# Attention slices spread over a block of feed-forward, engine latency in the planner, and a new order for the last output unit

## The chip, the cores and the metric

The kernel runs on one core of a Trainium2 chip. The metric is the device time of one execution in microseconds (us), as the median of a few runs. The engines are named as in the profile: PE is the tensor engine's matmul, PEld its weight loads, DVE the vector engine, ACT the scalar engine, POOL GpSimd, and SP the engine whose queue issues most stores.

## The reference

Linear attention of 8 batches, 8 heads, 576 tokens and 64 columns per head, normed, and then a bilinear feed-forward layer over all 4608 tokens:

```python
kv  = np.einsum('bhsd,bhse->bhde', k, v)
out = np.einsum('bhsd,bhde->bhse', q, kv)
rms = np.sqrt(np.mean(out * out, axis=-1, keepdims=True) + 1e-06)
x   = (out / rms * g_norm)            # (8, 8, 576, 64), then as (4608, 512)
a, b = x @ w_a, x @ w_b               # 512 x 1536 each
result = (a * b) @ w_out              # 1536 x 512
```

## The kernel before, in words

The feed-forward layer runs over nine blocks of 512 tokens. Block 0 is computed plainly (`std_block`, and `o_std` for its output in four products of 128 tokens, L815). Blocks 1 to 8 use Winograd's form of a 2x2 matrix product: seven products instead of eight, at the price of sums. In `wino_block` a block has six units `j`, each with the products p1 to p7 (four matmuls of 256 columns each, two for w_a and two for w_b, L718), evictions by ACT (`ev`, L411, to `u` or `c`), sums by DVE (`comb`, L737, to `c`), and a product a*b by DVE (`mul`, L771, to `abt`). Ahead of a block, DVE computes four differences of the normed tokens, m3, m1, m2 and m4 (`t_op`, L687, to `T` and `xp`), each of which reads the one before. The output of a block, `o_unit`, is the same form again: four sums of `abt` in two chunks (L866, to `as` and `abt`, a chain of four per chunk), seven products (L881, twelve matmuls each, in two pieces of six, in the last unit in six of two), evictions (L915) and sums (L921) to `o_sb`, and stores by SP (L788). It is worked off within the next block.

Attention of batch b makes the tokens that the blocks read. `load_node` brings q, k and v by GpSimd's DMAs, one batch behind the other (a copy to `gate_t`, L551, waits for the batch before), and a transposing DMA on SP makes `qT` (L570). `late_batch` copies the keys to another order (`kr_t` from `k_t`, L512, on DVE), multiplies keys and values (L521), and then works off eight slices, one for each pair of heads and half of the tokens: a matmul (L340), a square on ACT (L350), a matmul with ones (L354), a reciprocal root on ACT (L358), and a multiplication on DVE that writes the tokens to `xp` (L363).

All this is put in order by a planner when the program is built. Each piece of work is a `Node` with an engine, a duration, a priority, dependencies, and the buffers that it takes and frees; `Plan.order` then takes, again and again, the node that could start first by its own reckoning, and within 0.06 us the one with the smaller priority. The program's instructions stand on each engine in that order, and the engines run them in it. A dependency across engines counts with a latency from the table `LAT`; one on the same engine counts with none. The priority of a batch's work comes from its window, `at_win[b]`, two times between which its slices are spread evenly; `st` are the reckoned starts of the blocks. PSUM's banks go round in rings: 0 to 3 for the products (`RX`, `RY`), 4 for the output (`RO`), 5 to 7 for attention (`RQ`, `RS`).

Of the kernel before, what the change touches and what calls it, by code (L numbers as in the profile page):

```python
# [69 lines left out]

class Plan:
    LAT = {"PE": 0.27, "SP": 2.2, "ACT": 0.2, "DVE": 0.18}

    def __init__(self, t0):
        self.t0, self.nodes = t0, []
# [15 lines left out]
    def ready(self, n):  # L91
        t = 0.0
        for d, lat in n.deps:
            if d.end is None:
                return INF
            t = max(t, self.after(d, 0.0 if lat is None and d.eng == n.eng else lat))
        for b in n.takes:
            t = max(t, b.ring.when(), b.ring.pool.pick()[0])
        return t
# [35 lines left out]
def kernel(  # L135
# [11 lines left out]
    nc = tc.nc  # L147
# [10 lines left out]
    NCH = S // 128  # L158
# [275 lines left out]

    blocks_of = [(0, N0)] + [(t, t + 2 * n) for t, n in BLOCKS]
    readers = {}
    o_reads = []

    def slices(at, win, extra):
        w0, w1 = win  # L440
# [57 lines left out]
    def late_batch(b, load, win):  # L498
        at = Attn(b)
        w0, w1 = win  # L500
        kb, vb, qb = load["k"], load["v"], load["q"]
        kr, kd = Buf(RKR), Buf(RKD)
        at.qt = [qb, kd]

        def view(t):
            return t[:, 0 : H * (NCH + 1) * D].rearrange("p (h c d) -> p h c d", h=H, d=D)

        s = Buf(RS)

        r = plan.add(  # L510
            "DVE", 0.75, w0,
            lambda: nc.vector.tensor_copy(kr.tile[:], view(kb.tile).rearrange("p h c d -> p c h d")),  # L512
            [(load["n"], load["k_us"])], [kr], [kb],
        )

        def kv_mm():
            kv_ps = s.tile[:].rearrange("p (a e) -> p a e", a=NP)
            for c in range(NCH + 1):
                for p in range(NP):
                    hs = slice(2 * p, 2 * p + 2)  # L520
                    nc.tensor.matmul(  # L521
                        kv_ps[:, p, :],
                        lhsT=kr.tile[:, c, hs, :],
                        rhs=view(vb.tile)[:, hs, c, :],
                        start=(c == 0 and p == 0),
                        stop=(c == NCH and p == NP - 1),
                    )

        n = plan.add(
            "PE", 1.15, w0, kv_mm, [r, (load["n"], load["kv_us"]), plan.at(w0 - 3)], [s, kd], [kr, vb]  # L530
        )

        def kv_out():
            kv_ps = s.tile[:].rearrange("p (a e) -> p a e", a=NP)
            at.kvd = kd.tile
            nc.scalar.copy(at.kvd[0:D, :, 0:D], kv_ps[0:D, :, 0:D])
            nc.scalar.copy(at.kvd[D:, :, D:], kv_ps[D:, :, D:])
            for p in range(NP):
                at.q[p] = qb.tile[:, p, :]

        m = plan.add("ACT", 0.75, w0, kv_out, [n], (), [s])
        slices(at, (w0 + 0.12 * (w1 - w0), w1), lambda p: [m, (load["qn"], 5.5)])
# [127 lines left out]
    def wino_block(bi, win, wsum):  # L670
# [26 lines left out]
        for j in range(NJ):  # L697
# [16 lines left out]
            def pe(off, ps, lhs, rhs, start, deps, takes=(), frees=()):  # L714
                def prod():
                    for i, (w, sm) in enumerate(wts):
                        for kc in range(2):
                            nc.tensor.matmul(  # L718
                                ps.tile[:, i * n : (i + 1) * n],
                                lhsT=lhs(w, sm)[:, kc, :],  # L720
                                rhs=rhs()[:, kc, :],
                                start=start and i == 0 and kc == 0,
                                stop=kc == 1,
                                skip_group_check=True,
                            )

                return plan.add("PE", mm_us(4, n), pr + off, prod, deps, takes, frees)
# [13 lines left out]
            def w_at(kc, fs):  # L741
                return lambda w, sm: w[:, kc : kc + 2, fs]
# [4 lines left out]
            s1, s2, s3, s4 = ([wsum[w, j][i] for w in "ab"] for i in range(4))  # L747
            p1 = pe(0.0, X, w_at(0, fs), lambda: b11, True, xdeps(lo, t0, t0 + n), [X])
            e1 = ev(0.0, u1, X, p1)
            p2 = pe(0.1, Y, w_at(2, fs), lambda: b21, True, xdeps(hi, t0, t0 + n), [Y])  # L750
            c11 = comb(0.1, 0, 0, Y, u1, [p2, e1], [Y, u1])
            p6 = pe(0.2, X, s_at(0), lambda: tt(t2), False, [e1, m2] + s2, (), [t2])
            e2 = ev(0.2, u2, X, p6)
            p5 = pe(0.3, Z, w_at(0, f2), lambda: b12, True, [m1] + s1, [Z])
            p7 = pe(0.4, X, s_at(1), lambda: tt(t3), False, [e2, m3] + s3, (), [t3])
            e3 = ev(0.4, u3, X, p7)
            c22 = comb(0.4, 1, 1, Z, u3, [p5, e3], [u3])
# [16 lines left out]
            muls[j] = muls[j + NJ] = m  # L774
        return ab, muls

    def store(g0, o_sb):
        i = 0
        while i < 128:
            b, j = divmod(g0 + i, S)  # L780
            if b < NE:
                c, sp = divmod(j, EP)
                n = min(128 - i, EP - sp)
                r0, st = b * S + EC * sp + c, EC
            else:
                n = min(128 - i, S - j)
                r0, st = b * S + j, 1
            nc.sync.dma_start(out=out[r0 : r0 + st * (n - 1) + 1 : st, :], in_=o_sb[i : i + n, :])  # L788
            i += n

    def o_block(bi, ab, muls, osum, win, chunks, rings, pieces):
# [48 lines left out]
    def o_unit(r0, ab, muls, osum, pr, du, chunks, pieces, m, w, first, second, X, Y, Z, ob, s2, s3, s4, W):  # L840
# [83 lines left out]
                "DVE", dve_us((subs.stop - subs.start) * EH), pr + off * du, add, deps, (), frees  # L924
            )

        def put(fi, subs, deps, us=0.45):
            def go():
                for i in range(subs.start, subs.stop):
                    store(r0 + (fi * m + i) * 128, ob.tile[:, fi * m + i])  # L930

            plan.add("SP", us * (subs.stop - subs.start), pr + 7 * du, go, deps, (), [ob])

        b11, t1 = wo_t[:, 0:NJ, 0:EH], wo_t[:, 0:NJ, EH:]
        b21, b22 = wo_t[:, NJ:, 0:EH], wo_t[:, NJ:, EH:]
# [2 lines left out]
        if W is not None:  # L938
            u5 = Buf(RU)
            p1 = prod(0, X, a11, b11, True, [], [X])  # L940
            e1 = ev(0, 0, 0, p1, [ob])
            p2 = prod(1, Y, a12, b21, True, [], [Y])
            c11 = comb(1, 0, 0, Y, [p2, e1], [Y])
            p5 = prod(2, Z, a21, t1, True, [n1], [Z], (), 1)
            e5 = plan.add(
                "ACT", act_us(m * EH), pr + 2 * du,
                lambda: nc.scalar.copy(u5.tile[:, every], bank(Z, every)), [p5], [u5],
            )
            p3 = prod(3, Z, sx(s4), b22, False, [e5, n4], (), [s4], 3)
            p6 = prod(4, X, sx(s2), t2, False, [e1, n2], (), [s2], 2)  # L950
            e2 = ev(4, 0, 1, p6)
            c12 = comb(4, 0, 1, Z, [p3, e2], [Z])
            put(0, every, [c11, c12])
            p7 = prod(5, X, sx(s3), t3, False, [e2, n3], (), [s3], 0)
            e3 = ev(5, 1, 0, p7)
            c22 = comb(5, 1, 1, X, [p7], [X], u=u5)
            prod(6, W, a22, t4, True, [n4], [W], per_sub=ends)
            for i in range(m):
                subs = slice(i, i + 1)
                c21 = comb(6 + 0.1 * i, 1, 0, W, [ends[i], e3], [W], subs)  # L960
                put(1, subs, [c21, c22])
            return
        p1 = prod(0, X, a11, b11, True, [plan.at(46.5)], [X])
        e1 = ev(0, 0, 0, p1, [ob])
# [23 lines left out]
    at_win = {1: (34.5, st[1] - 3)}  # L988
    for b in range(2, B):
        t = b * S / N0  # L990
        at_win[b] = (max(61.0, st[int(t) - 1] + (t % 1) * L[int(t) - 1] - 10), st[int(t)] - 9 + (t % 1) * 12)
    loads = {2: load_node(2, 24.5, None)}
    for b in range(3, B):
        loads[b] = load_node(b, at_win[b - 1][0], loads[b - 1])
# [56 lines left out]
```

## Time and profile before

| what | us |
|---|---|
| median of 3 runs | 319.59 (319.47 to 319.6) |
| the profiled execution | 319.43 |
| its span, from the first to the last instruction | 317.6 |
| PE busy | 298.4 |
| DVE busy | 246.4 |
| ACT busy | 194.0 |
| POOL busy | 62.2 |
| granted clock of PE | 0.998 of full speed |

A row of the profile's groups names a line, an engine, an operation and its tiles (out<-in), the busy time, the mean in ns of one, and the idle time just before them with what ended most of it. A row of the timeline has the start, the length, and in brackets the idle time before it. Busy PE time includes the end of each matmul (0.27 us long, of which the next one covers the last part), so a stop shows as less idle time than it costs.

### The profile page before, as it was taken

The numbers are of one execution on the slowest core, as the hardware profiler recorded it, in microseconds if no ns is written. First come the engines' busy times: TensorE is split into PE (matmuls) and PEld (weight loads), VectorE is DVE, ScalarE is ACT, GpSimd is POOL, SyncE is SP. The second block draws the span as 40 slices with busy tenths as digits, with TensorE's granted clock in tenths as the row PEclk, the third lists the DMA queues.
The fourth block names the chain that finished last, engine by engine and source line by source line (L and its number), as shares of the span: only waits on it lengthen the run. The fifth ranks groups of instructions, "written<-read, shape, count | busy, mean of one in ns | idle before, by whom it ended". The sixth has DMA issues, their size and how long they took to land.

```text
span 317.6 us, 6672 instructions
## 1 busy us (share of the span) xinstructions
PE 298.4 (94%) x2631; PEld 238.6 (75%) x2631; DVE 246.4 (78%) x436; ACT 194.0 (61%) x403; POOL 62.2 (20%) x78
## 2 busy tenths in 40 slices
PE   8989899999899999999999999998999799999992
PEld 3534454886678888888788789887888688888882
DVE  4333875799996999789969986996699958997852
ACT  3754564686667764787469646875677465664511
POOL 8855800440707016004300000000000000000000
PEclk9999999999999999999999999999999999999999
DMA  8999999999998999916991500120013001100033
GB/s 161 190 198 200 199 194 187 179 155 170 98 182 74 181 201 84 141 68 145 80 141 68 126 18 2 51 83 2 2 26 109 1 2 66 68 3 0 34 101 132
DMA packets 80095, 32.72 MB, mean 103 GB/s; under 512 B 51904, under 2 KB 75456, under 8 KB 80064
## 3 DMA queue, kind: packets, MB, share of 16 engines
q0 software_dynamic: 59888, 18.44, 53.9%
q1 hardware_dynamic: 19968, 13.57, 17.0%
q8 instruction: 20, 0.33, 0.4%
q10 hardware_dynamic: 208, 0.29, 0.3%
q14 instruction: 11, 0.09, 0.1%
HBM read 37.75 MB, written 12.98 MB: 160 GB/s over the span
## 4 chain that ended last, share of the span: by engine, by line
PE 62%; DVE 25%; DMA 5%; issue 3%; ACT 3%; POOL 2%; DVEq 0%; ACTq 0%; POOLq 0%
PE bk L718 32%; PE bk L881 17%; DVE c L737 8%; PE bk L374 6%; DVE as L866 4%; DVE abt L771 4%; DMA abt<-in_q_dram 3%; DVE xp L363 3%; PE bk L817 2%; DMA as<-in_k_dram 2%; DVE T L687 2%; PE bk L340 2%; PE bk L354 1%; DVE abt L866 1%; DVE kr_t L512 1%
## 5 line engine op out<-in xcount | busy, mean ns | idle before, releaser
L737 DVE TENSOR_TENSOR c<-bk,u 128x512 f16<-128x512 f32 x144 | 96.6, 684 | 27.5 <-PE bk L718 16.8
L411 ACT COPY u<-bk 128x512 f32<-128x512 f32 x144 | 82.2, 589 | 42.9 <-PE bk L718 38.8
L718 PE MATMUL bk<-xp,wa_t 128*128 128x256 f16 x288 | 55.0, 272 | 1.8 <-DVE c L737 1.4
L718 PE MATMUL bk<-xp,wb_t 128*128 128x256 f16 x288 | 54.9, 272 | 0.0
L718 PEld LDWEIGHTS <-wa_t 128*128 128x128 f16 x384 | 37.3, 98 | 10.8 <-issue 4.9
L881 PEld LDWEIGHTS <-abt 128*128 128x128 f16 x384 | 37.6, 98 | 6.1 <-issue 0.9
L718 PEld LDWEIGHTS <-wb_t 128*128 128x128 f16 x384 | 37.5, 98 | 4.5
L363 DVE SCALAR_TENSOR_TENSOR xp<-bk,g_col,rs 128x288 f16<-128x288 f32 x64 | 32.6, 511 | 9.6 <-ACT rs L358 9.5
L718 PE MATMUL bk<-T,sa 128*128 128x256 f16 x192 | 36.6, 272 | 2.0 <-DVE T L687 2.0
L411 ACT CAST c<-bk 128x512 f16<-128x512 f32 x48 | 28.0, 588 | 16.0 <-PE bk L718 15.5
L881 PE MATMUL bk<-wo_t,abt 128*128 128x256 f16 x288 | 36.8, 273 | 1.0 <-DVE c L737 0.6
L358 ACT ACTIVATE rs<-bk,eps_t 128x288 f32<-128x288 f32 x64 | 32.4, 506 | 8.5 <-PE bk L354 8.1
L718 PE MATMUL bk<-T,sb 128*128 128x256 f16 x192 | 36.7, 273 | 0.0
L771 DVE TENSOR_TENSOR abt<-c 128x1024 f16<-128x1024 f16 x48 | 33.2, 692 | 4.3
L718 PEld LDWEIGHTS <-sa 128*128 128x128 f16 x288 | 28.1, 98 | 10.3 <-issue 6.4
L881 PEld LDWEIGHTS <-as 128*128 128x128 f16 x288 | 28.2, 98 | 5.3 <-issue 1.9
L718 PEld LDWEIGHTS <-sb 128*128 128x128 f16 x288 | 28.1, 98 | 3.3
L915 ACT COPY o_sb<-bk 128x512 f32<-128x512 f32 x31 | 18.2, 587 | 17.8 <-PE bk L881 17.5
L350 ACT ACTIVATE sq<-bk 128x288 bf16<-128x288 f32 x64 | 25.8, 414 | 3.5 <-PE bk L340 3.4
L881 PE MATMUL bk<-so,as 128*128 128x256 f16 x192 | 25.4, 272 | 1.4 <-ACT o_sb L915 1.3
L921 DVE TENSOR_TENSOR o_sb<-bk,o_sb 128x512 f32<-128x512 f32 (+1 forms) x25 | 16.4, 663 | 6.1 <-ACT o_sb L915 3.7
L554 POOL DMA_DIRECT2D scr<-in_q_dram x12 | 19.6, 1639 | 3.1 <-issue 2.4
(96 smaller groups left out, 393.6 us busy)
## 6 DMA issues: line engine op xcount, KB each, us to landing
out_dram<-o_sb SPq DMA_DIRECT2D x24, 256.0 KB, 2.3
scr<-in_q_dram POOLq DMA_DIRECT2D x12, 288.0 KB, 6.5
k_t<-in_k_dram POOLq DMA_DIRECT2D x6, 512.0 KB, 8.1
v_t<-in_v_dram POOLq DMA_DIRECT2D x6, 512.0 KB, 10.4
wo_t<-in_moe_w_out_dram POOLq DMA_DIRECT2D x2, 768.0 KB, 14.4
out_dram<-o_sb SPq DMA_DIRECT2D x12, 128.0 KB, 2.6
wa_t<-in_moe_w_a_dram POOLq DMA_DIRECT2D x5, 256.0 KB, 10.7
wb_t<-in_moe_w_b_dram POOLq DMA_DIRECT2D x5, 256.0 KB, 10.8
```

What stands on the lines that cost most here:

```text
L350: nc.scalar.activation(sq, self.x_ps[p, h][:, 0:HF], AF.Square)
L358: nc.scalar.activation(rs, self.s_ps[p, h][:, 0:HF], AF.Abs_reciprocal_sqrt, bias=eps_t)
L363: nc.vector.scalar_tensor_tensor(out=xcols(p, self.b * S + h * HF, HF), in0=self.x_ps[p, h][:, 0:HF], scalar=g_col, in1=self.rs[p, h], op0 ...
L374: nc.tensor.matmul(ps[:, 0:n], lhsT=w[:, kc, fc * 128 : (fc + 1) * 128], rhs=xcols(kc, 0, n), start=(kc == 0), stop=(kc == KC - 1),)
L411: ("ACT", act_us(n), lambda: nc.scalar.copy(*args())),
L554: nc.gpsimd.dma_start(out=scr[:, :, hl, :].rearrange("p s d -> s p d"), in_=qv[hl])
L718: nc.tensor.matmul(ps.tile[:, i * n : (i + 1) * n], lhsT=lhs(w, sm)[:, kc, :], rhs=rhs()[:, kc, :], start=start and i == 0 and kc == 0, st ...
L737: lambda: nc.vector.tensor_add(cs(fi, h), full(ps), u.tile),
L771: nc.vector.tensor_mul(t, c[:, :, :, 0], c[:, :, :, 1])
L881: nc.tensor.matmul(ps.tile[:, sub * EH : (sub + 1) * EH], lhsT=lhs(slice(j, j + 1))[:, 0, sub * 128 : (sub + 1) * 128], rhs=rhs[:, j, :], ...
L915: lambda: nc.scalar.copy(o(fi, h), bank(X, every)), [dep], takes, frees,
L921: nc.vector.tensor_add(o(fi, h, subs), bank(ps, subs), other)
```

## The change

It has five parts.

1. `Plan.OWN`: a dependency within ACT counts 0.12 us, within DVE 0.13 us, where it counted nothing.
2. The copy of the keys is cut in two, chunks 0 and 1 and then chunks 2 to 4, with a cost of its own each (0.08 + 0.265 per chunk, where the whole had 0.75). The second is behind the first.
3. In `wino_block`, p2 of a unit comes behind p5 of the unit before (an entry in the planner's dependencies).
4. In the last output unit (the one with a bank `W` of its own for p4), p6 moves ahead of p5, and p3 from the fourth place to behind p7; each 128 tokens' store is a node by itself, and SP and ACT issue two of the four each.
5. The windows: batches 2 to 7 start 8 us earlier and end 13 us earlier, by the planner's times, so that a batch's slices lie over the block rather than at its end. For batch 2 the start stays at 61.0 by the `max`, the end comes ahead of it, and its slices run from the last to the first.

```diff
+    OWN = {"ACT": 0.12, "DVE": 0.13}
...
-            t = max(t, self.after(d, 0.0 if lat is None and d.eng == n.eng else lat))
+            t = max(t, self.after(d, self.OWN.get(n.eng, 0.0) if lat is None and d.eng == n.eng else lat))
...
-        r = plan.add(
-            "DVE", 0.75, w0,
-            lambda: nc.vector.tensor_copy(kr.tile[:], view(kb.tile).rearrange("p h c d -> p c h d")),
-            [(load["n"], load["k_us"])], [kr], [kb],
-        )
+        def reorder(c0, c1, takes, frees):
+            return plan.add(
+                "DVE", 0.08 + 0.265 * (c1 - c0), w0,
+                lambda: nc.vector.tensor_copy(
+                    kr.tile[:, c0:c1], view(kb.tile)[:, :, c0:c1].rearrange("p h c d -> p c h d")
+                ),
+                [(load["n"], load["k_us"])], takes, frees,
+            )
+
+        r1 = reorder(0, 2, [kr], [kb])
+        r = reorder(2, NCH + 1, [], [kb])
+        r.deps.append((r1, None))
...
-            p2 = pe(0.1, Y, w_at(2, fs), lambda: b21, True, xdeps(hi, t0, t0 + n), [Y])
+            p2 = pe(0.1, Y, w_at(2, fs), lambda: b21, True, xdeps(hi, t0, t0 + n) + p5s[-1:], [Y])
...
             p5 = pe(0.3, Z, w_at(0, f2), lambda: b12, True, [m1] + s1, [Z])
+            p5s.append(p5)
...
-            nc.sync.dma_start(out=out[r0 : r0 + st * (n - 1) + 1 : st, :], in_=o_sb[i : i + n, :])
+            queue.dma_start(out=out[r0 : r0 + st * (n - 1) + 1 : st, :], in_=o_sb[i : i + n, :])
...
-            p5 = prod(2, Z, a21, t1, True, [n1], [Z], (), 1)
+            p6 = prod(2, X, sx(s2), t2, False, [e1, n2], (), [s2], 2)
+            e2 = ev(2, 0, 1, p6)
+            p5 = prod(3, Z, a21, t1, True, [n1], [Z], (), 1)
             e5 = plan.add(
-                "ACT", act_us(m * EH), pr + 2 * du,
+                "ACT", act_us(m * EH), pr + 3 * du,
                 lambda: nc.scalar.copy(u5.tile[:, every], bank(Z, every)), [p5], [u5],
             )
-            p3 = prod(3, Z, sx(s4), b22, False, [e5, n4], (), [s4], 3)
-            p6 = prod(4, X, sx(s2), t2, False, [e1, n2], (), [s2], 2)
-            e2 = ev(4, 0, 1, p6)
-            c12 = comb(4, 0, 1, Z, [p3, e2], [Z])
-            put(0, every, [c11, c12])
-            p7 = prod(5, X, sx(s3), t3, False, [e2, n3], (), [s3], 0)
-            e3 = ev(5, 1, 0, p7)
-            c22 = comb(5, 1, 1, X, [p7], [X], u=u5)
+            p7 = prod(4, X, sx(s3), t3, False, [e2, n3], (), [s3], 0)
+            e3 = ev(4, 1, 0, p7)
+            c22 = comb(4, 1, 1, X, [p7, e5], [X, u5], u=u5)
+            p3 = prod(5, Z, sx(s4), b22, False, [e5, n4], (), [s4], 3)
+            c12 = comb(5, 0, 1, Z, [p3, e2], [Z])
+            for i in range(m):
+                put(0, slice(i, i + 1), [c11, c12], queue=("SP", "ACT")[i])
             prod(6, W, a22, t4, True, [n4], [W], per_sub=ends)
             for i in range(m):
                 subs = slice(i, i + 1)
                 c21 = comb(6 + 0.1 * i, 1, 0, W, [ends[i], e3], [W], subs)
-                put(1, subs, [c21, c22])
+                put(1, subs, [c21, c22], queue=("ACT", "SP")[i])
...
-        at_win[b] = (max(61.0, st[int(t) - 1] + (t % 1) * L[int(t) - 1] - 10), st[int(t)] - 9 + (t % 1) * 12)
+        at_win[b] = (max(61.0, st[int(t) - 1] + (t % 1) * L[int(t) - 1] - 18), st[int(t)] - 22 + (t % 1) * 12)
```

What this does to the order shows on DVE. (The lines of the changed kernel have moved: L745 is L737 before, L780 is L771, L876 is L866, L695 is L687, L364 is L363, L514 is L512, L931 is L921.) First the end of block 5, where its last product `abt1` is made, before:

```order
L771 TENSOR_TENSOR abt1_88<-c1_92 128x2x512
L866 TENSOR_TENSOR as_90<-abt1_88 128x768
L866 TENSOR_TENSOR abt1_88<-abt1_88 128x3x256
L866 TENSOR_TENSOR as_90<-abt1_88 128x768
L866 TENSOR_TENSOR as_90<-abt1_88,as_90 128x768
L363 SCALAR_TENSOR_TENSOR xp1_80<-bk7_72,g_col_135,rs0_97 128x288
L687 TENSOR_TENSOR T_89<-xp1_80,xp0_79 128x512
L687 TENSOR_TENSOR xp0_79<-xp0_79 128x2x256
L687 TENSOR_TENSOR T_89<-xp1_80,xp0_79 128x512
L687 TENSOR_TENSOR T_89<-xp1_80,T_89 128x512
L363 SCALAR_TENSOR_TENSOR xp1_80<-bk6_71,g_col_135,rs1_98 128x288
L737 TENSOR_TENSOR c1_92<-bk0_65,u_93 128x512
```

And the same place now:

```order
L780 TENSOR_TENSOR abt1_88<-c1_92 128x2x512
L745 TENSOR_TENSOR c0_91<-bk1_66,u_93 128x512
L876 TENSOR_TENSOR as_90<-abt1_88 128x768
L745 TENSOR_TENSOR c1_92<-bk0_65,u_93 128x512
L876 TENSOR_TENSOR abt1_88<-abt1_88 128x3x256
L745 TENSOR_TENSOR c0_91<-bk1_66,u_93 128x512
L876 TENSOR_TENSOR as_90<-abt1_88 128x768
L780 TENSOR_TENSOR abt0_87<-c0_91 128x2x512
L876 TENSOR_TENSOR as_90<-abt1_88,as_90 128x768
L931 TENSOR_TENSOR o_sb1_101<-bk2_67,o_sb1_101 128x2x256
```

The four output sums, which stood behind each other, alternate with the sums of the wino products; the slices' L363 and the four of T stand earlier, among the units of block 5. The next place is the copy of batch 3's keys, in block 1, before:

```order
L866 TENSOR_TENSOR as_90<-abt1_88,as_90 128x768
L512 COPY kr_t_84<-k_t_81 128x2560
L627 TENSOR_TENSOR wo_t_75<-wo_t_75 128x6x256
L737 TENSOR_TENSOR c0_91<-bk1_66,u_93 128x512
L771 TENSOR_TENSOR abt1_88<-c0_91 128x2x512
L627 TENSOR_TENSOR so_78<-wo_t_75 128x1536
L363 SCALAR_TENSOR_TENSOR xp1_80<-bk7_72,g_col_135,rs2_99 128x288
L737 TENSOR_TENSOR c1_92<-bk3_68,u_93 128x512
```

And now:

```order
L514 COPY kr_t_84<-k_t_81 128x1024
L876 TENSOR_TENSOR as_90<-abt1_88 128x768
L745 TENSOR_TENSOR c0_91<-bk2_67,u_93 128x512
L364 SCALAR_TENSOR_TENSOR xp0_79<-bk5_70,g_col_135,rs0_97 128x288
L514 COPY kr_t_84<-k_t_81 128x1536
L364 SCALAR_TENSOR_TENSOR xp0_79<-bk6_71,g_col_135,rs1_98 128x288
L745 TENSOR_TENSOR c0_91<-bk2_67,u_93 128x512
L876 TENSOR_TENSOR abt1_88<-abt1_88 128x3x256
```

The copy is in two parts with other work between them, and the sums of w_out's parts (L627, to `wo_t` and `so`) have moved some thirty instructions ahead. Last, the end of the program, before:

```order
L866 TENSOR_TENSOR as_90<-abt0_87,as_90 128x512
L921 TENSOR_TENSOR o_sb1_101<-bk1_66,o_sb1_101 128x2x256
L921 TENSOR_TENSOR o_sb0_100<-bk0_65,o_sb0_100 128x2x256
L921 TENSOR_TENSOR o_sb0_100<-bk2_67,o_sb0_100 128x2x256
L921 TENSOR_TENSOR o_sb0_100<-bk4_69,u_93 128x2x256
L921 TENSOR_TENSOR o_sb0_100<-bk5_70,o_sb0_100 128x256 x2
```

And now:

```order
L876 TENSOR_TENSOR as_90<-abt0_87,as_90 128x512
L931 TENSOR_TENSOR o_sb0_100<-bk3_68,o_sb0_100 128x2x256
L931 TENSOR_TENSOR o_sb0_100<-bk4_69,u_93 128x2x256
L931 TENSOR_TENSOR o_sb0_100<-bk6_71,o_sb0_100 128x256
L931 TENSOR_TENSOR o_sb0_100<-bk1_66,o_sb0_100 128x2x256
L931 TENSOR_TENSOR o_sb0_100<-bk6_71,o_sb0_100 128x256
```

The sum of p7 with p5 (`bk4_69` with `u_93`) comes second instead of last but one, and the sum of p3 (`bk1_66`) moves between the two halves of p4 (`bk6_71`).

More of the change, by code (lines that the diff above doesn't have):

```diff
@@ L436 @@
     readers = {}
-    o_reads = []
+    o_reads, p5s = [], []
     def slices(at, win, extra):
@@ L775, in wino_block, with store @@
         return ab, muls
-    def store(g0, o_sb):
+    def store(g0, o_sb, queue=None):
+        queue = queue or nc.sync
         i = 0
@@ L925, in comb, with put @@
             )
-        def put(fi, subs, deps, us=0.45):
+        def put(fi, subs, deps, us=0.45, queue="SP"):
+            q = {"SP": nc.sync, "ACT": nc.scalar}[queue]
             def go():
                 for i in range(subs.start, subs.stop):
-                    store(r0 + (fi * m + i) * 128, ob.tile[:, fi * m + i])
-            plan.add("SP", us * (subs.stop - subs.start), pr + 7 * du, go, deps, (), [ob])
+                    store(r0 + (fi * m + i) * 128, ob.tile[:, fi * m + i], q)
+            plan.add(queue, us * (subs.stop - subs.start), pr + 7 * du, go, deps, (), [ob])
         b11, t1 = wo_t[:, 0:NJ, 0:EH], wo_t[:, 0:NJ, EH:]
```

## The prediction, made before the changed kernel was run

> **What bounds the kernel now.** I read the busy times first, then the span in stretches, then who the tensor engine waited for, and last the instructions around its longest stops.
>
> ```profile
> PE 298.4 (94%) x2631; PEld 238.6 (75%) x2631; DVE 246.4 (78%) x436; ACT 194.0 (61%) x403; POOL 62.2 (20%) x78
> ```
>
> The tensor engine (PE) is busy nearly always, so only its stops and the two ends can be won. The stretches below have PE's busy time as their second figure, DVE's as the fourth.
>
> ```profile
> core 0: us, PE busy (x) PEld busy (x) DVE busy (x) ACT busy (x) POOL busy (x), PEclk, DMA share, GB/s
> 57.00:76.00 19.00, 19.00 (x171) 15.72 (x170) 16.55 (x28) 14.45 (x31) 6.56 (x7) 1.00 1.44 173
> 76.00:99.00 23.00, 20.22 (x182) 16.64 (x181) 22.09 (x37) 16.55 (x37) 8.34 (x9) 1.00 1.14 129
> ...
> 99.00:144.00 45.00, 44.41 (x410) 39.01 (x409) 37.95 (x67) 31.26 (x65) 11.41 (x13) 1.00 1.08 130
> 144.00:156.00 12.00, 11.84 (x113) 9.93 (x111) 11.62 (x21) 7.40 (x15) 3.44 (x3) 1.00 1.13 138
> ...
> 172.00:186.00 14.00, 12.69 (x110) 10.46 (x108) 12.66 (x24) 9.79 (x20) 0.00 (x0) 1.00 0.46 119
> 186.00:213.00 27.00, 27.00 (x255) 23.79 (x253) 21.83 (x37) 18.21 (x39) 0.00 (x0) 1.00 0.11 39
> 213.00:219.00 6.00, 4.52 (x41) 3.75 (x39) 5.62 (x12) 2.42 (x6) 0.00 (x0) 1.00 0.01 4
> ...
> 244.00:253.00 9.00, 7.24 (x62) 5.78 (x60) 8.62 (x18) 4.89 (x11) 0.00 (x0) 1.00 0.00 1
> ```
>
> PE stops where one block of tokens gives way to the next, and there DVE is 90 to 97% busy. The waits of PE from 60 to 300 us say the same: DVE's results, or the output's evictions.
>
> ```profile
> PE bk L718 <- DVE c L737: 2.1, 5, 0.6
> PE bk L718 <- DVE T L687: 2.0, 3, 0.9
> ```
>
> One such place, block 5 to 6: PE first, then ACT, then DVE.
>
> ```profile
> 213.84 1.47 PE L881 MATMUL bk<-wo_t,abt 128*128 128x256 f16 x12
> 215.99 1.47 PE L881 MATMUL bk<-so,as 128*128 128x256 f16 x12 [0.68 <-ACT o_sb L915]
> 218.26 0.38 PE L718 MATMUL bk<-T,sa 128*128 128x256 f16 x2 [0.81 <-DVE T L687]
> ```
> ```profile
> 215.35 0.59 ACT L915 COPY o_sb<-bk 128x512 f32<-128x512 f32 x1 [0.88 <-PE bk L881]
> ```
> ```profile
> 214.07 0.56 DVE L866 TENSOR_TENSOR as<-abt 128x768 f16<-128x768 f16 x1
> ...
> 215.85 0.56 DVE L866 TENSOR_TENSOR as<-abt,as 128x768 f16<-128x768 f16 x1
> ...
> 216.87 0.43 DVE L687 TENSOR_TENSOR T<-xp,xp 128x512 f16<-128x512 f16 x1
> ...
> 218.25 0.43 DVE L687 TENSOR_TENSOR T<-xp,T 128x512 f16<-128x512 f16 x1
> ```
>
> Output products p1 and p6 stand behind each other, so p6 waits for the eviction of p1; then PE waits for the chain of T, which DVE reaches only after four L866. Twelve matmuls take 1.47 us with the last one's 0.27, so matmuls start 0.109 us apart; the next could start at 215.15 and starts at 215.99. A stop thus costs its printed idle and 0.16 more. Counted over all starts in this way, PE loses 15.4 us after 57 us: 4.2 in 76 to 99, 1.4 in 99 to 144, 1.6 in 144 to 156, 2.2 in 172 to 186, 1.8 in 213 to 219, 2.5 in 244 to 253, and 1.7 scattered. That is the most that a better order can win there.
>
> **The prices on DVE.**
>
> ```profile
> 294.41 0.42 DVE L866 TENSOR_TENSOR as<-abt,as 128x512 f16<-128x512 f16 x1
> 294.75 0.42 DVE L866 TENSOR_TENSOR as<-abt 128x512 f16<-128x512 f16 x1
> 295.20 0.42 DVE L866 TENSOR_TENSOR abt<-abt 128x512 f16<-128x512 f16 x1
> ```
> ```profile
> L737 DVE TENSOR_TENSOR c<-bk,u 128x512 f16<-128x512 f32 x144 | 96.6, 684 | 27.5 <-PE bk L718 16.8 <-ACT u L411 10.5
> L771 DVE TENSOR_TENSOR abt<-c 128x1024 f16<-128x1024 f16 x48 | 33.2, 692 | 4.3
> L363 DVE SCALAR_TENSOR_TENSOR xp<-bk,g_col,rs 128x288 f16<-128x288 f32 x64 | 32.6, 511 | 9.6 <-ACT rs L358 9.5
> L866 DVE TENSOR_TENSOR as<-abt 128x768 f16<-128x768 f16 x28 | 15.5, 554 | 0.6
> L512 DVE COPY kr_t<-k_t 128x2560 bf16<-128x2560 bf16 x6 | 8.8, 1475 | 0.0
> L687 DVE TENSOR_TENSOR T<-xp,xp 128x512 f16<-128x512 f16 x16 | 6.7, 421 | 0.4
> L627 DVE TENSOR_TENSOR so<-wo_t 128x1536 f16<-128x1536 f16 x2 | 1.9, 950 | 0.0
> ```
>
> The second L866 starts 0.34 us after the first, which it doesn't read, the third 0.45 after the second, whose result it reads. So an instruction occupies DVE for its mean less 0.08, and 0.12 more where its successor reads it. In the two orders, 111 DVE instructions before and 45 now stand directly behind the one that they read: 66 x 0.12 = 7.9 us of DVE time saved.
>
> The Trainium skill, "VectorE: DVE Perf Modes", section "The DRAIN you can't avoid", speaks against this gain: the next operation waits for the pipe in any case, eight copies take as long with a semaphore after each as without, and the count of operations is what to cut. By that rule the 66 pairs save nothing and six more copies only cost. The 0.34 and 0.45 above disagree with it as far as the dependence goes. What it would make of the time is the second rival.
>
> **The change part by part**, in us of PE's time.
>
> Blocks 5 to 6 and 6 to 7: lost 1.8 + 2.5 = 4.3. In the new order p2 (12 x 0.109) and two wino products (4 x 0.109 each) stand between the last piece of p1 and the first of p6: 2.2 us against a copy of 0.59. All eight slices of batch 6 are done two units before the boundary, so T is computed ahead of it, and the L866 alternate with the combs. I leave 0.8: 3.5 won. Ends: 4.3 (no stop), 1.8 (both stops of p6 go, 2 x 0.84, and T's stay).
>
> Blocks 3 to 4 and 4 to 5: lost 3.8, the same pile of four L866, T, the last slices and a key copy. All are spread now, but the slices run through the first half of the block and the key copy stands near the boundary. I take a little over half: 2.1. Ends 3.4 and 0.5.
>
> Block 1 to 2, lost 4.2. From the fourth product (L771) of block 1 to the second of block 2, DVE has before: 8 L363 x 0.43, 11 L737 x 0.60, 6 L866 x 0.47, 2 L512 x 1.39, 3 L627 x 0.87, 4 L771 x 0.61, 4 L687 x 0.34, one output sum x 0.60, and 10 dependent pairs x 0.12: 23.8, against 20.7 of matmul pitches there. Now: 11 L363, 8 L866, no L627 (they stand earlier, behind the fourth plain output product), the key copies in two parts, no dependent pair, the rest alike. A part more costs 0.08: L866 takes 0.55 for 768 columns and 0.42 for 512, so 0.15 is fixed, and about half of it is overlapped; I reckon 1.48 for both parts. That makes 22.4 against 21.1. DVE's excess falls from 3.1 to 1.3; I take 1.6 of the 1.8. Ends: 3.0 and -1.5, since batch 3's slices now start beside batch 2's last ones, which run backwards: block 2's first product needs slice 0, now the last.
>
> The rest, lost 3.1: 0.3 won, ends 1.5 and -1.5. New small stops: the slices are now spread over the units of each block; one that delays an eviction costs PE some 0.2, and I set 0.7 against that (ends 0 and 3).
>
> The fourth plain output product moves from the midst of block 1 to just behind the other three, and the first now stands in this stop (0.30 + 0.16):
>
> ```profile
> 48.03 0.28 PE L354 MATMUL bk<-sq,ones 128*128 128x288 bf16 x1 [0.30 <-ACT sq L350]
> ```
>
> I take 0.3 (ends 0.46 and -0.3, if w_out's load is late for it). The loads:
>
> ```profile
> 78.33 0.18 POOL L551 COPY gate_t<-qT 1x1 bf16<-1x1 bf16 x1 [11.50 <-DMA qT<-scr]
> ...
> 86.11 0.29 PE L340 MATMUL bk<-qT,kvd 128*128 128x288 bf16 x1
> ```
>
> Batch 3's queries are there at 78.3 and were first used at 86.1. That use moves ahead by 3.1 us of matmuls and the stops removed before it, to about 81: 2.7 spare, nothing to pay. If that cover goes, PE waits for the transpose. GpSimd's order is unchanged. On SP two stores of the fourth plain output tile now stand ahead of batch 3's transpose instead of behind it; the tile is ready earlier too, so I cost that at nothing. Holding p2 behind the unit before's p5 is a rule for the planner alone and adds no wait on the chip; what it does to the order is in the counts above. Behind the two stores on ACT's queue nothing else stands.
>
> The end:
>
> ```profile
> 310.46 1.47 PE L881 MATMUL bk<-so,as 128*128 128x256 f16 x12
> ...
> 311.96 0.59 ACT L915 COPY o_sb<-bk 128x512 f32<-128x512 f32 x1 [1.56 <-PE bk L881]
> ...
> 312.58 0.69 DVE L921 TENSOR_TENSOR o_sb<-bk,u 128x512 f32<-128x512 f32 x1 [1.45 <-ACT o_sb L915]
> 313.19 0.74 DVE L921 TENSOR_TENSOR o_sb<-bk,o_sb 128x256 f32<-128x256 f32 x2
> ```
> ```profile
> 312.00:313.00 1.00, 0.00 (x0) 0.00 (x0) 0.42 (x1) 0.55 (x1) 0.00 (x0) 1.00 1.00 373
> ```
> ```profile
> out_dram<-o_sb SPq DMA_DIRECT2D x24, 256.0 KB, 2.3
> ```
>
> Behind the last matmul (ended 311.94) stand a copy, a sum of 0.69 and two half sums: the last result comes 2.0 later, at 313.93, and its store, behind another on SP, is issued at 314.1 and lands 2.3 later, 4.5 after PE's end. Now p7, p3 and half of p4 come last. A full sum, which can start 0.44 before PE's end, and a half sum are left, so the last result comes 0.6 after it, 1.4 sooner. But three of the four 256 KB stores are then issued within half a microsecond, the first 0.3 after PE's end. DMA moves 373 GB/s at a share of 1.00, 0.7 us a store: they land 2.6, 3.3 and 4.0 after PE's end. So 0.5 is won (ends 1.4 and 0).
>
> The Trainium skill, "DMA: Bandwidth & Descriptors", section "Issuing engines are not separate DMA queues", says that a second issuing engine saves only the issue time; by it the end wins 0.5 and the sum stays at 311.8; if each queue moved its stores for itself, 1.4 and 310.9. The share of 1.00 with one queue agrees with it.
>
> Sum: 3.5 + 2.1 + 1.6 + 0.3 - 0.7 + 0.3 + 0.5 = 7.6, set against the profiled execution's 319.43 (317.6 of span and 1.8 around it; the median 319.59 is 0.16 above): 311.8.
>
> **Rivals.** First, more: the stops feed on one backlog, and once DVE keeps pace everywhere nearly all go. With 4 of 15.4 left, 11.4 + 0.3 + 0.5: 307.2. For it: 186 to 213, where DVE is busy 81% of the time, shows no idle PE. Against: slices run now where none ran.
>
> Second, less: dependent neighbours cost DVE nothing that PE sees, and the stops come back as waits for banks. Then block 1 to 2 gives 0, blocks 3 to 5 give 0.9, and 5 to 7 only p6's 1.8: with 0.8 for the two ends of the kernel, 0.3 for the rest and the 0.7 against, 3.1 won: 316.3. For it: with T's wait gone, L737's waits lead the list. Against: the 0.34 and 0.45 above.
>
> Third, no change: the stops only change place, as DVE's total falls by 3% alone. For it: 246 of 317 us are much for a queue in fixed order. 319.4.
>
> Fourth, slower: in the units, where six slices of batch 2 cost PE nothing visible before (57 to 76), each of the 48 slices of batches 2 to 7 now delays an eviction. At 0.3 each that is 14.4 against 8.3 won without the 0.7: 325.5. It decides from 8.3 / 48 = 0.17 a slice. Against: 99 to 144 holds 14 slices of batches 3 and 4 and loses 1.4, 0.1 each.
>
> **Numbers.** Forecast 0.50 (309 to 314.5), more 0.18, less 0.21, no change 0.04, slower 0.07. The range runs from 307.5 to 317, which holds all but the far ends of the first two rivals and the last two. Faster by over 0.2% 0.88, within 0.2% (about what a measurement here can tell from none) 0.04, slower 0.08.
>
> **What would show it.** In the profile after: no wait of PE for T or for L915 above 0.4 at the boundaries of blocks 5 to 7; DVE's busy share in those stretches under 90%; L866 rarely 0.59 apart; block 1 to 2 still the worst stretch; the last sum within 0.7 of the last matmul, and stores with a DMA share near 1.00 to within 0.5 us of their end. It is wrong if PE's idle in unit middles grows to several microseconds, if queries (L340) are waited for on a DMA, or if block 1 to 2 loses over 6.

## The result, and the profile after

The changed kernel takes 309.12 us (median of 4 runs, 307.96 to 311.27), the one before 319.53 (319.25 to 319.6): a ratio of 0.968 [0.963, 0.974]. 10.4 us are won; 7.6 had been forecast. The profiled execution took 307.96, the quickest of the four, with a span of 306.2 and a granted clock of 1.00. Of two kernels further below, one execution each (315.7 and 313.19 us, over 1.5% above the fastest of its kernel) stands in no ratio.

The busy times, as shown of before, and of the waits of PE from 60 to 300 us the first two:

```profile
PE 294.4 (96%) x2629; PEld 238.7 (78%) x2631; DVE 240.0 (78%) x442; ACT 192.6 (63%) x403; POOL 63.1 (21%) x78
```
```profile
PE bk L726 <- DVE c L745: 1.0, 1, 1.0
PE bk L341 <- DVE xp L364: 0.6, 2, 0.5
```

No wait for the chain of T is left, and none for the output's eviction. The sums `c`, five waits before, are one wait now, and that one is new, as shown below. DVE is 6.4 us less busy. Of 68 output sums (L866, now L876) 25 started 0.58 or 0.59 us behind another of them before, and 5 do now.

The span in stretches (PE's busy time is the second figure, DVE's the fourth); block 2 begins at 82.1 us, block 6 at 202.7, block 7 at 233.8:

```profile
core 0: us, PE busy (x) PEld busy (x) DVE busy (x) ACT busy (x) POOL busy (x), PEclk, DMA share, GB/s
...
76.00:95.00 19.00, 17.72 (x161) 14.50 (x159) 18.63 (x38) 15.06 (x35) 6.58 (x7) 1.00 1.29 131
...
109.00:116.00 7.00, 5.98 (x65) 5.29 (x64) 4.88 (x9) 4.32 (x10) 0.00 (x0) 1.00 1.40 197
116.00:138.00 22.00, 22.00 (x201) 19.44 (x200) 19.93 (x39) 16.48 (x36) 7.69 (x7) 1.00 1.33 143
...
200.00:206.00 6.00, 6.00 (x63) 5.45 (x61) 5.75 (x11) 3.25 (x7) 0.00 (x0) 1.00 0.48 177
206.00:231.00 25.00, 25.00 (x235) 22.27 (x233) 20.54 (x38) 18.61 (x41) 0.00 (x0) 1.00 0.04 8
231.00:237.00 6.00, 6.00 (x57) 5.38 (x56) 6.00 (x14) 3.75 (x8) 0.00 (x0) 1.00 0.43 147
```

At the start of blocks 6 and 7 DVE is as full as before, 5.75 of 6 us and 6.00 of 6, and yet PE has no idle time there. The reason stands in DVE's rows at the start of block 6. All slices are done by 200.3, and the four sums of T (L695) lie between others, the last ending at 204.2, where before PE waited 0.81 for them:

```profile
198.09 0.41 DVE L695 TENSOR_TENSOR T<-xp,xp 128x512 f16<-128x512 f16 x1
198.42 0.55 DVE L876 TENSOR_TENSOR as<-abt 128x768 f16<-128x768 f16 x1
198.89 0.42 DVE L695 TENSOR_TENSOR xp<-xp 128x512 f16<-128x512 f16 x1
...
199.82 0.51 DVE L364 SCALAR_TENSOR_TENSOR xp<-bk,g_col,rs 128x288 f16<-128x288 f32 x1
...
203.78 0.43 DVE L695 TENSOR_TENSOR T<-xp,T 128x512 f16<-128x512 f16 x1
```

What remains in the middle is one stop near 112 us, seen on POOL, DVE and PE:

```profile
102.92 0.90 POOL L569 DMA_DIRECT2D k_t<-in_k_dram  x1
...
112.45 0.43 DVE L514 COPY kr_t<-k_t 128x1024 bf16<-128x1024 bf16 x1 [2.12 <-DMA k_t<-in_k_dram]
```
```profile
113.53 0.38 PE L726 MATMUL bk<-xp,wa_t 128*128 128x256 f16 x2 [1.02 <-DVE c L745]
```

DVE stands 2.12 us in front of the copy of batch 5's keys, whose load landed some 9.5 us after its issue. The sum that PE needs is behind that copy. The engine named in PE's bracket is DVE, but the cause is a DMA that DVE's queue waits for.

The end of the kernel:

```profile
299.70 0.69 DVE L931 TENSOR_TENSOR o_sb<-bk,u 128x512 f32<-128x512 f32 x1 [3.80 <-ACT o_sb L925]
300.31 1.53 DVE L931 TENSOR_TENSOR o_sb<-bk,o_sb 128x256 f32<-128x256 f32 x3
300.77 0.60 PE L891 MATMUL bk<-so,abt 128*128 128x256 f16 x4 [0.42 <-DVE o_sb L931]
300.81 0.91 ACTq L798 DMA_DIRECT2D out_dram<-o_sb  x2
```
```profile
303.00:304.00 1.00, 0.00 (x0) 0.00 (x0) 0.00 (x0) 0.00 (x0) 0.00 (x0) 1.00 1.03 383
304.00:304.50 0.50, 0.00 (x0) 0.00 (x0) 0.00 (x0) 0.00 (x0) 0.00 (x0) 1.00 0.89 336
304.50:305.00 0.50, 0.00 (x0) 0.00 (x0) 0.00 (x0) 0.00 (x0) 0.00 (x0) 1.00 0.01 0
```

The last sum ends at 301.84, 0.47 after the last matmul; the stores run at a share of 1.0 until about 304.5. There is a new stop here too: the second half of p4 waits 0.42 until DVE has read the first half, which lies in the same bank of PSUM.

Counted over all starts of PE as in the prediction, the loss after 57 us fell from 15.4 to 5.8. The rest of the difference between the two spans (11.4) is 0.4 at the start, 0.5 for the fourth plain output product, and 0.9 behind the last matmul's start.

### The profile page after: what moved, and what is told of

It reads as the page before. It is cut to its first block, busy times and chain, and to the rows that moved or that the text cites. A ratio compares the mean times of both kernels' runs of the same rounds, so it can differ in the third digit from the quotient of the medians.

```text
span 306.2 us, 6682 instructions
## 1 busy us (share of the span) xinstructions
PE 294.4 (96%) x2629; PEld 238.7 (78%) x2631; DVE 240.0 (78%) x442; ACT 192.6 (63%) x403; POOL 63.1 (21%) x78
## 4 chain that ended last, share of the span: by engine, by line
PE 60%; DMA 31%; POOL 3%; issue 2%; DVE 1%; ACT 0%; POOLq 0%; SPq 0%; DVEq 0%
PE bk L726 36%; PE bk L891 20%; DMA scr<-in_q_dram 10%; DMA qT<-scr 10%; DMA abt<-in_k_dram 4%; DMA k_t<-in_k_dram 3%; DMA abt<-in_q_dram 3%; DMA as<-in_k_dram 2%; POOL scr L562 2%; PE bk L355 1%; PE bk L341 1%; PE bk L529 1%; POOL wa_t L287 1%; POOL wb_t L288 1%; DVE o_sb L931 1%
## 5 line engine op out<-in xcount | busy, mean ns | idle before, releaser
L745 DVE TENSOR_TENSOR c<-bk,u 128x512 f16<-128x512 f32 x144 | 96.6, 685 | 23.3 <-ACT u L412 12.2
L364 DVE SCALAR_TENSOR_TENSOR xp<-bk,g_col,rs 128x288 f16<-128x288 f32 x64 | 32.6, 511 | 11.5 <-ACT rs L359 11.1
L780 DVE TENSOR_TENSOR abt<-c 128x1024 f16<-128x1024 f16 x48 | 32.8, 686 | 1.6
L355 PE MATMUL bk<-sq,ones 128*128 128x288 bf16 x64 | 18.3, 286 | 1.1 <-ACT kvd L323 0.6
## 6 DMA issues: line engine op xcount, KB each, us to landing
v_t<-in_v_dram POOLq DMA_DIRECT2D x6, 512.0 KB, 11.2
```

What stands on the lines that cost most here:

```text
L355: nc.tensor.matmul(ps[:, 0:HF], lhsT=ones, rhs=self.sq[p, h], start=True, stop=True)
L364: nc.vector.scalar_tensor_tensor(out=xcols(p, self.b * S + h * HF, HF), in0=self.x_ps[p, h][:, 0:HF], scalar=g_col, in1=self.rs[p, h], op0 ...
L745: lambda: nc.vector.tensor_add(cs(fi, h), full(ps), u.tile),
L780: nc.vector.tensor_mul(t, c[:, :, :, 0], c[:, :, :, 1])
```

## The experiments

Two theories stood against each other. W: the stops at the starts of blocks go because the slices and the sums of T have left those places, that is, by the windows. D: they go because the planner's latency keeps instructions that read each other apart, so that DVE keeps pace. The first kernels put one part each into the kernel before, and then two.

**Windows alone.**

```diff
-        at_win[b] = (... - 10), st[int(t)] - 9 + (t % 1) * 12)
+        at_win[b] = (... - 18), st[int(t)] - 22 + (t % 1) * 12)
```

> The kernel before with the new windows alone (part 5); planner's latency, key copy, p2 and last unit as before. Theory W (the boundaries clear because the slices' work and T have left them): batch 6's slices and T are now ahead of the last unit of block 5 in the order, so the stops of blocks 3 to 7 (8.1 us of 15.4) nearly go, block 1 to 2 keeps its 4 and the tail stays: about 312.5. Theory D (DVE keeps pace because dependent pairs are no longer neighbours): 106 pairs of 111 are left, so most stops stay in other places: about 317.

Measured: 314.99 (314.18 to 316.18), ratio 0.987 [0.984, 0.989], some 4.4 us won: between the two.

**Latency alone**, with the rule on p2. The rule belongs to it: with the latency and without the rule the planner comes to a state where no node can go, because two units hold each other's banks.

```diff
+    OWN = {"ACT": 0.12, "DVE": 0.13}
...
+            p2 = pe(... xdeps(hi, t0, t0 + n) + p5s[-1:], [Y])
```

> The kernel before with the planner's latency within ACT and DVE (part 1) and the rule that p2 comes behind p5 of the unit before (part 3), which the planner needs to end at all with that latency; windows, key copy and last unit as before. 45 dependent pairs instead of 111. Theory W: T of blocks 5 to 7 is still 3 to 9 instructions behind the last product of the block before and 2 or 3 slices too, so the stops there stay or halve: about 317.5. Theory D: 66 x 0.12 us of DVE time, about 312.

Measured: 312.62 (312.15 to 312.89), ratio 0.979 [0.977, 0.980], 6.8 won: D's number. What the rule does alone wasn't tried.

**The last unit alone.**

> The kernel before with the new last output unit and the stores on two queues alone (part 4). Both theories: nothing moves ahead of 300 us; the end comes sooner. By the prediction 0.5, by the trace after 0.9 less the two stops of 0.5 there: 318.6 to 319.2. If the two queues moved their data side by side: 318.

Measured: 318.27 (317.86 to 318.73), ratio 0.997 [0.996, 0.998]: 0.9 won, with 0.5 to 1.4 in the interval. That is more than the 318.6 to 319.2 expected, and near the 318 of two queues that move their data side by side. The kernel with one queue, below, speaks against that reading.

**Windows and latency.**

> The kernel before with windows, latency and the p2 rule (parts 1, 3 and 5), key copy in one and the old last unit. Theory W: little more than the windows alone, about 311.5. Theory D: little more than the latency alone, about 311. If both are needed together: 310.5, that is all of the gain but the tail's 0.5 and the key copy's share at block 1 to 2, where batch 3's slices now wait on the whole copy: 1 us worse than the changed kernel there.

Measured: 310.39 (308.89 to 310.99), ratio 0.971 [0.968, 0.974]. Together they win 9.1, and not the 11.2 of the sum of both. The interval is clear of those of either part alone, so each adds to the other; the time doesn't tell the 310.5 from D's 311.

Then the other way round: the changed kernel with one part undone.

**Without the windows.**

> The changed kernel with the old windows (part 5 undone); 39 dependent pairs on DVE. Theory W (the boundaries clear because the slices' work and T have left them): the piles are back, T of block 7 is 9 instructions behind the last product: 316.5. Theory D (DVE keeps pace because dependent pairs are no longer neighbours): 311.

Measured: 310.83 (310.38 to 311.24), ratio 0.974 [0.972, 0.976]. D's number.

**Without the latency.**

> The changed kernel without the latency within ACT and DVE in the planner (part 1 undone); 107 dependent pairs. Theory W: the boundaries stay clear, block 1 to 2 gets 1 to 2 us worse: 311. Theory D: 7.4 us of DVE time are back, about 316.

Measured: 311.38 (310.77 to 312.44), ratio 0.977 [0.975, 0.979]. W's number: the first of these two goes against W, the second against D. The changed kernel itself, run beside them:

> The changed kernel itself once more, with the same chip as the three that undo a part: 308 to 311.3 as before. If its spread comes from the loads (the key copy of batch 5 waited 2.1 us for its DMA at 112 and PE 1.0 for that), this profile shows that wait longer or shorter with the time; if from the clock, the granted clock does.

Measured: 310.08 (308.91 to 311.67), ratio 0.972 [0.968, 0.976]. The profiled execution, 1.5 us longer than that of the first comparison, has the longer wait: 2.61 us for the load and 1.51 of idle PE behind it, where it was 2.12 and 1.02. Its granted clock is 0.998 against 1.000. The intervals of the two kernels with a part undone overlap with this one, so by the time alone neither part is shown to matter once the other is in. Undoing the windows also removes the stop at the key copy (a loss of 0.1 from block 2 to 3, in the table below, where the copy stands at 116.8 us and doesn't wait), which hides part of its price.

Neither theory holds for the whole. What each part does was to be read by place. The table has PE's loss in the profiled execution of each kernel, counted like the 15.4, each column from the middle of one block to the middle of the next. "Pairs" are DVE instructions that stand directly behind the one they read, counted in the order.

| kernel | 1 to 2 | 2 to 3 | 3 to 5 | 5 to 7 | 7 to end | sum | pairs | median us |
|---|---|---|---|---|---|---|---|---|
| before | 3.9 | 1.7 | 4.0 | 5.0 | 0.8 | 15.4 | 111 | 319.5 |
| windows alone | 3.8 | 1.4 | 2.6 | 1.7 | 1.0 | 10.4 | 106 | 315.0 |
| latency alone | 3.0 | 1.0 | 2.3 | 2.7 | 0.1 | 9.1 | 45 | 312.6 |
| windows and latency | 3.1 | 2.5 | 1.0 | 0.1 | 0.6 | 7.4 | 47 | 310.4 |
| after, no windows | 3.1 | 0.1 | 1.1 | 3.5 | 0.1 | 7.8 | 39 | 310.8 |
| after, no latency | 3.8 | 0.8 | 1.0 | 1.6 | 1.6 | 8.7 | 107 | 311.4 |
| after | 2.8 | 1.3 | 0.4 | 0.1 | 1.2 | 5.8 | 45 | 309.1 |

The start of block 2 answers to the latency alone (3.8 and 3.9 without it, 2.8 to 3.1 with it). In the column from block 5 to 7 either part leaves 1.6 to 3.5, and both leave 0.1. But a column takes in half a block on both sides of each start. From the first product of a block to the first one that reads T, counted in the same way, PE lost at blocks 6 and 7:

| kernel | block 6 | block 7 |
|---|---|---|
| before | 1.9 | 2.3 |
| latency alone | 0.9 | 1.7 |
| after, no windows | 1.7 | 1.7 |
| windows alone | 0.0 | 0.0 |
| after, no latency | 0.1 | 0.1 |
| windows and latency; after | 0.0 | 0.0 |

So the windows alone clear these starts, as W says, and those of blocks 4 and 5 too (0.3 and 0.7 before, nothing with the windows alone). What is left with the windows and without the latency is a stop of 0.7 some 9 us into block 7 and small ones; with the latency added they are gone. The stretch from 205 to 242 us, first of the changed kernel without the windows and then without the latency (the latter has a stop of 0.7 just behind it):

```profile
205.00:242.00 37.00, 34.86 (x322) 30.32 (x321) 30.13 (x56) 24.74 (x53) 0.00 (x0) 1.00 0.10 30
```
```profile
205.00:242.00 37.00, 37.00 (x345) 32.65 (x343) 32.75 (x58) 25.64 (x54) 0.00 (x0) 1.00 0.14 44
```

What the windows do there shows in the first of these two, on DVE and PE at the start of block 6:

```profile
206.13 0.51 DVE L364 SCALAR_TENSOR_TENSOR xp<-bk,g_col,rs 128x288 f16<-128x288 f32 x1
...
208.09 0.41 DVE L695 TENSOR_TENSOR xp<-xp 128x512 f16<-128x512 f16 x1
```
```profile
208.55 0.38 PE L726 MATMUL bk<-xp,wa_t 128*128 128x256 f16 x2 [1.25 <-DVE xp L695]
```

The slices reach to 206.6, the chain of T comes behind them, and PE waits 1.25 us for it. With the windows moved, the slices were done 2.4 us ahead of the block.

**The key copy in one piece**, all else as changed.

> The changed kernel with the key copy in one piece (part 2 undone), at the planner's old cost of 0.75. Where the halves let other sums through, block 1 to 2 is to lose 1 to 1.5 us more: 310.3. If the split is worth nothing: 309.1.

Measured: 309.34 to 312.37 in three executions, ratio 0.973 [0.969, 0.978]. That isn't told apart from the changed kernel beside it (0.972), so the time doesn't show what the cut of the copy is worth. The table by place shows something. "After, no windows" differs from "latency alone", and "after" from "windows and latency", in the cut and in the last unit only, and the last unit changes nothing at blocks 3 to 5. There the loss is 1.1 against 2.3, and 0.4 against 1.0: the cut goes with 0.6 to 1.2 us at that place.

The changed kernel's loss from block 2 to 3 is nearly all the stop at the key copy, and its runs spread over 1%, where those of before spread over 0.1 to 0.4%. Four more kernels were to settle that and the end.

**The stores of the last unit all on SP.**

```diff
-                put(0, slice(i, i + 1), [c11, c12], queue=("SP", "ACT")[i])
+                put(0, slice(i, i + 1), [c11, c12], queue="SP")
...
-                put(1, subs, [c21, c22], queue=("ACT", "SP")[i])
+                put(1, subs, [c21, c22], queue="SP")
```

> The changed kernel with all stores of the last unit issued by SP, as before the change. Theory that the end is set by the transfers themselves (they run at the full DMA share until the end): the stretch from the last matmul's start to the end of the span stays within 0.3 us of the 5.1 that the changed kernel shows, and the time within 0.3 us of 309 to 310. Rival, that the second queue is what shortened the tail: the stretch goes back towards the 6.0 of before, and the time rises by 0.6 to 0.9 us.

Measured: 308.75 (308.17 to 310.91), ratio 0.969 [0.966, 0.972]. From the last matmul's start to the end of the span it is 5.04 us, against 5.09 with two queues. The issues and the stretch behind them:

```profile
301.05 1.89 SPq L798 DMA_DIRECT2D out_dram<-o_sb  x4
```
```profile
302.00:303.00 1.00, 0.00 (x0) 0.00 (x0) 0.09 (x1) 0.00 (x0) 0.00 (x0) 1.00 1.03 383
303.00:304.00 1.00, 0.00 (x0) 0.00 (x0) 0.00 (x0) 0.00 (x0) 0.00 (x0) 0.85 1.01 379
```

No gain of the second queue shows; the transfers are at a share of 1.0 with one. One profile each prices this to no better than 0.9 us: the next kernel, with two queues, has 5.98. The Trainium skill, "DMA: Bandwidth & Descriptors", section "Issuing engines are not separate DMA queues", says that a second issuing engine saves only the time of issuing, and 5.04 against 5.09 agrees with it.

**The key copy planned later.**

```diff
-            (16.0, 10.0, 14.0, 17.0) if dep is None else (7.0, 3.5, 7.0, 10.5)
+            (16.0, 10.0, 14.0, 17.0) if dep is None else (7.0, 3.5, 10.0, 10.5)
```

> The changed kernel with one number more changed: the planner takes the key load of a batch as 10 us instead of 7, so that it plans VectorE's key copy later. Theory that the stop of 1.2 us near 112 us is VectorE's queue standing behind a key copy whose load has not landed: no wait of VectorE's key copy on the load over 0.5 us near 112, no TensorE stop over 0.6 us between 100 and 145 us, 0.8 to 1.5 us less than the changed kernel (308.0 to 309.0), and repeats within 0.7 us of each other. Rival, that the copy only moves and the load chain holds the batch itself: a stop of the same size 10 us later, and the same time, 309.5 to 310.5. A second rival: the copy now comes late for the scores, and the stop is on the matmul that reads the copied keys.

Measured: 308.19 (307.09 to 308.48), ratio 0.965 [0.963, 0.967]. The copy of batch 5's keys now comes without a wait, and PE is busy throughout the place:

```profile
117.36 0.42 DVE L514 COPY kr_t<-k_t 128x1024 bf16<-128x1024 bf16 x1
```
```profile
109.00:116.00 7.00, 7.00 (x76) 6.34 (x74) 6.23 (x11) 4.59 (x11) 0.00 (x0) 1.00 1.32 226
```

The loss from block 2 to 3 is 0.1 instead of 1.3, and no stop came in its place: the theory of the load holds, both rivals fall. The spread, 1.4 us, is twice the 0.7 expected, by one run that was quicker than the others.

**Two banks for the last p4.**

```diff
-            W = Buf(rings[3]) if len(rings) > 3 else None
+            W = [Buf(rings[3]) for _ in range(m)] if len(rings) > 3 else None
```

> The changed kernel with the two halves of the last unit's fourth projection in two banks of PSUM, so that the matmuls of the second half need not stand behind VectorE's reading of the first. Theory that the stop of 0.58 us there (0.42 of it a wait for VectorE) comes from the shared bank, and that the stores set the end anyway: no wait for VectorE's last sum in the last 8 us, and a time 0 to 0.3 us lower. Rival, that the matmuls of the second half set the end: 0.5 us lower.

Measured: 311.85 (308.27 to 312.51), ratio 0.973 [0.969, 0.977]. The stop in p4 is gone, but in the profiled execution the key copy waited longer than in any other of these:

```profile
304.04 0.60 PE L893 MATMUL bk<-so,abt 128*128 128x256 f16 x4
```
```profile
114.76 0.43 DVE L514 COPY kr_t<-k_t 128x1024 bf16<-128x1024 bf16 x1 [4.05 <-DMA k_t<-in_k_dram]
```

So the time says nothing about the banks. The profile does: from the start of p3's twelve matmuls (302.73) to the end of the span it is 7.32 us, against 7.31 in the changed kernel, where p4 stops. The stores set the end, as expected, and the stop at p4 costs nothing there.

The time says a good deal about the load. Behind PE's stop of 2.94 us at the key copy the granted clock is 0.5 for 3.4 us, from 116.84 to 120.26, and two matmuls start 0.43 apart where it is 0.22 elsewhere:

```profile
115.84 0.38 PE L726 MATMUL bk<-xp,wa_t 128*128 128x256 f16 x2 [2.94 <-DVE c L745]
```
```profile
116.90:120.20 3.30, 3.30 (x17) 2.34 (x16) 2.56 (x5) 1.93 (x4) 0.00 (x0) 0.50 1.49 157
```

Of the 4.8 us lost from block 2 to 3, 3.1 are the stop and 1.7 this clock. Behind the stops of 1.02 and 1.51 us the clock stayed at 1.00. Among four kernels with the same order up to the last unit, the loss from block 2 to 3 and the time of the profiled execution go together:

| execution | key load issued at | copy begins | loss, 2 to 3 | time |
|---|---|---|---|---|
| after | 102.92 | 112.45 | 1.3 | 307.96 |
| one queue | 103.46 | 112.36 | 1.5 | 308.17 |
| after, again | 103.82 | 113.22 | 2.5 | 309.42 |
| two banks | 104.76 | 114.76 | 4.8 | 311.85 |

Of the 20 executions of these four kernels, the 9 above 310.5 us have a mean granted clock of 0.986 to 0.992, and the 11 below 309.5 one of 0.995 to 1.000. So the load and the clock go together in the long executions, and in the one that was profiled the lower clock came behind the stop. That it was so in the other eight isn't shown.

**Both.**

> The changed kernel with both of the last two edits. By the theories of the two, 0.8 to 1.8 us less than the changed kernel: 307.7 to 309.0, with one stop of TensorE over 0.5 us after 90 us (0.49 in the last unit), if any. Rival: the order moves again, and the stops come back at other places, 309.5 to 310.5.

Measured: 307.81 (307.36 to 307.96), ratio 0.9638 [0.962, 0.965], the lowest of all. Both stops are gone: PE's loss after 57 us is 3.9, against 4.5 with the key copy alone, from whose time (308.19) this one isn't told apart. From the start of p3 to the end of the span it is 8.17 us, against 8.20 there: again the second bank moves PE's end and not the kernel's. It is 1.3 us less than the changed kernel in the first comparison, where the intervals still overlap a little (0.963 to 0.974 there), and 2.3 less than in the second, where they don't (0.968 to 0.976).

## Why the prediction was right

The measured 309.12 lies at the lower edge of the forecast's own 309 to 314.5, and the sum of 311.8 is 2.7 too high: two of its terms were under-sized by 1.4 and 1.5. The mechanism held for the starts of blocks: the stops there go, and slices inside the units cost nothing visible. From 116 to 138 us and from 206 to 231, where eight and seven slices now run, PE has no idle time, so the decisive 0.17 a slice of the "slower" rival is far off.

The price of dependent neighbours held less well. The prediction drew its gain from 66 pairs at 0.12 us of DVE time, and DVE's time does fall with them: it is busy 244.8 us with 107 pairs (after, no latency) and 240.0 with 45 (after). But the windows cleared the starts of blocks 4 to 7 with the pairs in place. The latency alone, with the rule on p2, won 6.8 us, and it is what the start of block 2 and the small stops inside blocks answer to. The "less" rival's 316.3 falls. The reading of "The DRAIN you can't avoid" (the Trainium skill, "VectorE: DVE Perf Modes") by which the next operation waits for the pipe in any case doesn't fit the 0.34 between starts of operations 0.42 long; the section itself excepts a next operation that is not held. That PE's gain is the pairs' 0.12 each, and not that the planner with truer times also sets a better order, isn't shown: no run has the same order with and without the pairs.

By its terms, from the table by place, whose columns are a little wider than the prediction's stretches (before, they hold 5.0, 4.0 and 3.9 us for its 4.3, 3.8 and 4.2):

- Blocks 5 to 6 and 6 to 7: 4.9 won for 3.5 forecast. The 0.8 left in them is 0.1. The windows took the stops at the starts, and the latency what was left between them.
- Blocks 3 to 5: 3.6 won for 2.1, the term that was most under-sized. "A little over half" supposed that the slices' spread and the key copy would still cost something at the boundary. They cost 0.4. The stops at the starts are gone by the windows alone, and a part of the rest goes with the cut of the key copy.
- Block 1 to 2: 1.1 won for 1.6. The excess of DVE is the right picture (18.6 of 19 us busy), and it is still the place with the most loss that isn't a load's.
- The rest, 0.3 won, and new small stops, 0.7 lost: nothing won in sum, but by other means. 1.8 of the old loss went, and two new stops came, 1.2 at the key copy and 0.6 at p4's bank. The prediction saw neither. It looked at the spare of batch 3's queries and found 2.7 us. It didn't ask the same of batch 5's keys, whose copy stands in DVE's queue ahead of sums that PE needs; and it counted the halves of p4 as work in one bank without asking whether the second must wait for DVE's reading of the first.
- The fourth plain output product: 0.5 for 0.3.
- The end: 0.9 behind the last matmul's start, less the 0.6 at p4 that is counted above, is 0.3 for 0.5. The part alone gave 0.9 in time, with an interval (0.5 to 1.4) that takes in the forecast. The working (transfers bound it, not issues) is right; the last store landed 3.6 us behind PE's end, where the sum had 4.0 and the kernel before 4.5.

The signs were right for T, L915, L866, block 1 to 2 (but for the key copy's stop), the last sum, and the stores, whose share stays near 1.00 until 304.5, 0.5 ahead of the last landing at 304.96. None of the signs of being wrong came: the queries (L341) wait for no DMA, and block 1 to 2 loses 2.8. One sign failed. DVE's share in the stretches of blocks 6 and 7 is not under 90%: it is 96 and 100%. A full DVE didn't stop PE there, since what PE needed next stood early enough in its queue. From the last landing to the end of the span it is 1.2 us before and after. The landing itself varies: with the same last unit, the last store landed 3.07 us after its issue in one execution and 3.95 in another (key copy planned later), and the stretch from the last matmul's start to the end was 5.09 and 5.98. So one profile can't price the end to better than 0.9.

## What to carry to other kernels

Where a planner fixes the order ahead of time, put work that must be done by a boundary well ahead of it, which alone cleared the starts of blocks here, and let the planner count what the next instruction on the same engine really waits for: either alone left stops that both together removed. Before trusting a tightened order, ask of each instruction in a queue that waits for a load how much spare it had, since all that stands behind it shares the wait. A wider spread of runs is a sign of such a load: one number for the duration of the key loads took 1.2 us of loss away, and none of the eight executions with it took over 308.5.

## What was not expected of the hardware

The same program's loads arrived at different times: over four executions with the same order, batch 5's keys were issued between 102.92 and 104.76 us and could be copied 8.9 to 10.0 us later. The time went from 308 to 312 with it, in the longest of the four partly by the clock: a stop of 2.94 us was followed by 3.4 us at a granted clock of 0.5, which cost another 1.7. The gate ahead of them, which waits for batch 4's transposed queries, opened at 98.98 in the changed kernel and at 96.72 before, though the gate before it opened 0.2 us earlier than then. Why that transpose comes later wasn't tried.
